# Spectral filter and gated convolution: all eight batches relaid on chip by in-place transposes instead of through DRAM

## The chip, the cores and the metric

The kernel runs on one core of one Trainium2 chip. The metric is device time in microseconds (us) of one execution; the time of a kernel is the median of its runs. A time with a profile comes from one execution that the hardware profiler recorded, and its span runs from the first to the last instruction.

TensorE (PE) multiplies matrices from SBUF into PSUM, which has eight banks of 512 f32 per partition here. VectorE (DVE) and ScalarE (ACT) read PSUM, and copy results out of it. GpSimd (POOL) works on SBUF only and also issues DMAs, as does SyncE (SP). Each engine works through its own instructions in the order in which they were written.

## The reference

```python
def _attn_ref(x, filt_r, filt_i):               # x: (8, 3200, 256) float32
    X = np.fft.rfft(x, axis=1)                  # filters: (1601, 256)
    Y = X * (filt_r + 1j * filt_i)[None, :, :]
    return np.fft.irfft(Y, n=x.shape[1], axis=1)

def _moe_ref(x, w_val, conv_w, w_out):          # x is the result above
    gate_pre = ...                              # causal convolution, 5 taps per channel
    gate = 1.0 / (1.0 + np.exp(-gate_pre))
    return gate * (x @ w_val) @ w_out           # 256 x 256 weights
```

Each of eight batches is filtered along its 3200 positions in the frequency domain, and the result goes through a sigmoid gate (a five-tap convolution), a 256 x 256 product and an output product.

## The kernel before

The length 3200 is written as 100 x 32, so that each transform is two small ones with a relayout between them. One batch goes through these stages (the names are those of the functions and of the planner's tasks):

- `load_x` (L450, DMA issued on POOL): four loads of 100 x 8 x 256 into `xt`, converted to bf16.
- `s1` (L717, PE): eight pairs of matmuls with the cosine table; `so` copies each out of PSUM (ACT or DVE). `turn` (L736, DVE): four in-place transposes of 32 x 32 blocks of 32-bit words, each word two neighbouring channels in bf16. `s2` (L745, PE) in seven chunks, copied out to `xs`.
- `zed` (L765 or L768): the product with the filter, per chunk two multiplications of 128 x 1024 bf16 (the seventh chunk is half as wide). In batches 1 to 7 five chunks of seven are on POOL (L768) and two on DVE (L765); in batch 0 all are on DVE.
- `inva` (L778, PE): first inverse stage, seven chunks; `ue` copies each out of PSUM.
- The inverse relayout. In batches 1 to 7 `ue` copies to `u`, `wr` (L818) writes `u` to a DRAM scratch `escr` with seven DMAs, and `lv` (L825) reads it back in the other layout into `vt` with eight DMAs, all on SP's queue. `lv` waits for all seven writes. In batch 0 alone (`turned`) `ue` copies into the scratch tile `yt` in pieces of four channels, and `turn2` (L808, DVE) transposes to `vt` with four instructions that write each 32-bit word 512 bytes from the last.
- `ib` (L831, PE): 64 small matmuls whose weights are slices of `vt`; `ye` (L841, ACT) copies out to `yt`, the filtered signal.
- `conv` (L861), `gate` (L870, ACT), `val` (L877) and `gv` (L887, DVE), `outp` (L897) and `oe` (a copy to `o`), `store` (L916, L919, DMAs on SP).

All copies out of PSUM go through one helper, so they have the lines L443 (ACT) and L445 (DVE) and are told apart by their tiles. The helper `copy` is an ACTIVATE on ACT and a tensor copy on DVE.

The order on all engines is laid out ahead: `tasks` lists every piece of work with a cost, a rank (`period`, `off`, `step`, `set`, `move` in `CFG`), buffers that it takes and gives, and PSUM banks; `Plan.run` goes through time, always starts the ready task with the lowest rank on a free engine, and the code is emitted in that order. It also decides which copies go to ACT and which to DVE. Nothing is reordered at run time.

The table `ci_t` of the last inverse stage is computed near the start by some forty small POOL instructions (`ci_dve`, L642 to L691), in two variants, one for each layout of `vt`.

Of the kernel before, what the change touches and what calls it, by code (L numbers as in the profile page):

```python
# [39 lines left out]
    off=dict(lx=-8.88, s1=1.96, t1=3.63, s2=6.86, xs=21.17, z=1.67, ia=13.06, ue=3.93,  # L40
         t2=-19.97, wr=-19.93, lv=18.75, ib=22.57, ye=6.81, cv=37.79, ga=-0.5, vl=26.91,
         gv=22.89, op=11.0, oe=-2.84, st=22.73),
    step=dict(lx=1.84, s1=0.42, t1=3.74, t2=1.66, s2=0.13, xs=1.06, z=0.38, ia=0.73,
         ue=2.68, wr=0.9, lv=1.54, ib=0.85, ye=2.8, cv=3.99, ga=2.94, vl=1.98, gv=0.32,
         op=0.98, oe=3.24, st=4.45),
    dup=('SP', 'SP'),
    set=dict(ey=-16.46, tab=16.6, tabs=3.8, ci=7.23, dg=29.54, fd=-37.59, w=27.01),
    move={('cv', 0): 2.79, ('cv', 1): -11.55, ('cv', 2): -0.2, ('cv', 3): -1.85, ('cv', 4):
# [34 lines left out]
    stay=0,  # L83
    hold=4.78,
# [11 lines left out]
class Plan:  # L96
# [14 lines left out]
    def run(self):  # L111
# [28 lines left out]
        while left or any(lines.values()):  # L140
# [29 lines left out]
            if best is None:  # L170
                later = [ready_at[n] for n in ready if ready_at[n] > now + 1e-9]
                later += [v for v in free.values() if v > now + 1e-9]
                later += [g[0] for g in events if g[0] > now + 1e-9]
                live = [q for q in lines.values() if q]
                if live:
                    rate = 1.0 / len(live)
                    later.append(now + min(q[0][0] for q in live) / rate)
                assert later, ("stuck", sorted(ready)[:20], self.room, banks)
                then = min(later)
                for q in live:  # L180
                    q[0][0] -= (then - now) * rate
                    if q[0][0] <= 1e-9:
                        n, give = q.pop(0)[1:]
# [28 lines left out]
            if t["dma"]:  # L212
                lines[t["dma"][0]].append([t["dma"][1], n, t["give"]])
# [10 lines left out]
def tasks(cfg, B):  # L224
    plan = Plan(cfg["room"], cfg["stay"], cfg["hold"])
    turned, move = set(cfg["turned"]), cfg["move"]
# [14 lines left out]
    fixed("s1", {"POOL": 2.0}, -95, [], ("iota_b",))  # L241
# [12 lines left out]
    fixed("cid", {"POOL": 4.5}, sr["ci"], ["s1"], ("ci_dve",))  # L254
    fixed("cia", {"ACT": 0.6}, sr["ci"], ["cid"], ("ci_act",))
    fixed("cim", {"POOL": 0.5}, sr["ci"], ["cia"], ("ci_mul",))
    fixed("id", {"DVE": 0.6}, sr["ey"], ["s1"], ("eye32",))
    fixed("dg", {"ACT": 2.0}, sr["dg"], ["id"], ("diag",))
    for c, (m0, m1) in enumerate(FCUT):
        nm = m1 - m0  # L260
        for w in range(2):
            for t in range(2):
                for k in range(3):
                    fixed(f"f{c},{w},{t},{k}", {"POOL": 0.55}, -90 + c, [], ("fload", c, w, t, k),
                          dma=("SW", 0.53 if k == 0 else 0.065 * nm))
        for t in range(2):
            for w in range(2):
# [3 lines left out]
                      ("fdup", c, t, w), dma=("HW", 0.09 * nm) if by == "SP" else None)  # L271
    fixed("wl", {"POOL": 3.0}, sr["w"], [], ("wload",), dma=("SW", 1.2))
# [3 lines left out]
    for b in range(B):  # L276
        for c in range(NXC):
            add(f"lx{b},{c}", {"POOL": 0.7}, "lx", b, c if b else c - 100, [], ("load_x", b, c),
                take=("xt",), dma=("SW", 2.4))
# [7 lines left out]
        for q in range(4):  # L287
            add(f"t1{b},{q}", {"DVE": 1.16}, "t1", b, q, sos + ([f"t1{b},{q - 1}"] if q else []),
                ("turn", b, q))
        for u, (m0, nm) in enumerate(UCH):  # L290
# [8 lines left out]
            if u in cfg["pool_u"][min(b, 1)]:  # L299
                for w in range(2):  # L300
                    add(f"z{b},{u},{w}", {"POOL": 0.13 + 0.975 * nm}, "z", b, u,
# [14 lines left out]
            if b not in turned:
                add(f"wr{b},{u}", {"SP": 0.4}, "wr", b, u,
                    [f"ue{b},{u}"] + ([f"wr{b},{u - 1}"] if u else []), ("wr", b, u),
                    take=("e",) if u == 0 else (), give=("u",), dma=("HW", 0.45 * nm))
        if b in turned:  # L320
            for q in range(4):
                add(f"t2{b},{q}", {"DVE": 1.77}, "t2", b, q, [f"ue{b},{u}" for u in range(NU)]
                    + ([f"t2{b},{q - 1}"] if q else []), ("turn2", b, q),
# [639 lines left out]
```

## Time and profile before

| | us |
|---|---|
| median of three runs | 344.0 |
| the runs | 341.51, 344.0, 346.14 |
| the profiled execution | 341.4 |
| its span | 339.7 |
| PE, DVE, ACT, POOL busy in it | 270.1, 268.0, 243.4, 192.4 |

The span leaves 1.7 us of the execution outside it. The granted TensorE clock was 0.938 of full speed on the mean. In rows of the profile, a group shows line, engine, operation, output<-inputs, shapes and count, then busy us and mean ns of one, then the idle time of its engine just before them and what ended it.

### The profile page before, as it was taken

How to read it: one execution, taken by the hardware profiler on the slowest of the kernel's cores; microseconds unless marked ns; L12 is line 12 of the kernel's file. 1: busy time of each engine (PE TensorE's matmuls, PEld its weight loads, DVE VectorE, ACT ScalarE, POOL GpSimd, SP SyncE). 2: the span in 40 equal slices, each digit the busy share in tenths (PEclk: the TensorE clock that was granted, in tenths of full speed). 3: DMA queues.
4: the chain of work that ended last, by engine and by line, in shares of the span. 5: the costliest groups of instructions: out<-in, count | busy, mean ns of one | idle time of the engine just before them, and what ended most of it. 6: DMA issues, size and time to landing. Idle time of an engine off the chain costs nothing.

```text
span 339.7 us, 11239 instructions
## 1 busy us (share of the span) xinstructions
PE 270.1 (80%) x4804; PEld 165.0 (49%) x4804; DVE 268.0 (79%) x340; ACT 243.4 (72%) x318; POOL 192.4 (57%) x214
## 2 busy tenths in 40 slices
PE   2645387769778788977897979987889989989894
PEld 0133124445345443544445646645545666657663
DVE  4887477999999898995699669789997464877482
ACT  2984287968786775834996967896984979546864
POOL 8487885498995879858356540598499610000000
PEclk9999995899995897985998999999997999999999
DMA  6999869704579645999589716786684694687436
GB/s 110 167 209 218 181 87 192 128 20 159 182 224 234 157 152 183 273 221 248 200 178 301 213 67 217 273 285 213 186 261 173 220 309 145 226 298 282 179 138 249
DMA packets 47690, 67.57 MB, mean 199 GB/s; under 512 B 5209, under 2 KB 31705, under 8 KB 47641
## 3 DMA queue, kind: packets, MB, share of 16 engines
q1 hardware_dynamic: 40648, 51.79, 45.1%
q0 software_dynamic: 6992, 15.08, 25.3%
q8 instruction: 37, 0.61, 0.7%
q14 instruction: 13, 0.10, 0.1%
HBM read 42.08 MB, written 38.14 MB: 236 GB/s over the span
## 4 chain that ended last, share of the span: by engine, by line
PE 37%; DMA 25%; DVE 17%; ACT 9%; issue 7%; POOL 2%; SPq 1%; DVEq 0%; ACTq 0%; POOLq 0%
DMA vt<-escr 9%; PE ps L877 8%; PE ps L897 8%; DMA out_dram<-o 7%; DVE z L765 6%; PE ps L861 6%; ACT yt L841 6%; PE ps L717 5%; PE ps L778 4%; PE ps L831 4%; DMA f_t<-in_filt_i_dram 3%; DMA f_t<-in_filt_r_dram 3%; DVE vt L808 2%; DMA f_t<-f_t 2%; PE ps L745 2%
## 5 line engine op out<-in xcount | busy, mean ns | idle before, releaser
L768 POOL TENSOR_TENSOR z<-xs,f_t 128x1024 bf16<-128x1024 bf16 (+1 forms) x70 | 140.0, 2029 | 52.5 <-DVE xs L445 27.9
L887 DVE TENSOR_TENSOR gv<-ps,gt 128x512 bf16<-128x512 f32 (+1 forms) x112 | 65.4, 625 | 21.2 <-ACT gt L870 13.1
L870 ACT ACTIVATE gt<-ps 128x1024 bf16<-128x1024 f32 (+1 forms) x56 | 49.6, 934 | 22.7 <-PE ps L861 20.0
L877 PE MATMUL ps<-yt,wv_t 128*128 128x512 bf16 (+1 forms) x224 | 58.0, 368 | 6.0 <-DVE o L445 2.9
L841 ACT ACTIVATE yt<-ps 128x800 bf16<-128x800 f32 (+1 forms) x72 | 54.3, 783 | 8.0 <-PE ps L831 7.0
L897 PE MATMUL ps<-wo_t,gv 128*128 128x256 bf16 x384 | 57.6, 279 | 0.6 <-DVE o L445 0.3
L717 PE MATMUL ps<-xt,cf_t 100*128 100x512 bf16 x128 | 48.2, 483 | 12.0 <-DMA xt<-in_x_dram 10.6
L765 DVE TENSOR_TENSOR z<-xs,f_t 128x1024 bf16<-128x1024 bf16 (+1 forms) x42 | 51.0, 1257 | 5.4 <-DMA xt<-in_x_dram 3.9
L443 ACT ACTIVATE so<-ps 128x1024 bf16<-128x1024 f32 x43 | 42.7, 1029 | 8.6 <-PE ps L717 8.6
L897 PEld LDWEIGHTS <-gv 128*128 128x128 bf16 x384 | 40.0, 116 | 15.7 <-issue 5.9
L831 PE MATMUL ps<-ci_t,vt 104*128 104x100 f16 (+1 forms) x512 | 37.7, 227 | 8.9 <-DMA vt<-escr 4.9
L861 PE MATMUL ps<-yt,dg_t 32*32 32x512 bf16 (+1 forms) x2240 | 39.6, 363 | 5.7 <-issue 3.3
L443 ACT ACTIVATE u<-ps 128x1024 bf16<-128x1024 f32 (+1 forms) x33 | 31.7, 975 | 16.6 <-DMA escr<-u 8.4
L831 PEld LDWEIGHTS <-vt 104*128 104x128 bf16 (+1 forms) x512 | 31.8, 109 | 23.5 <-issue 8.2
L443 ACT ACTIVATE o<-ps 128x512 f32<-128x512 f32 (+1 forms) x58 | 33.2, 586 | 13.4 <-PE ps L897 10.2
L778 PE MATMUL ps<-z,a_t 64*64 64x256 bf16 x416 | 31.2, 302 | 13.6 <-ACT so L443 3.6
L445 DVE COPY o<-ps 128x512 f32<-128x512 f32 (+1 forms) x46 | 29.8, 661 | 12.9 <-PE ps L897 7.1
L736 DVE STREAM_TRANSPOSE so<-so 128x1024 f32<-128x1024 f32 x32 | 38.7, 1235 | 0.2
L778 PE MATMUL ps<-z,b_t 64*64 64x256 bf16 x416 | 30.0, 294 | 7.5 <-DVE z L765 7.5
L443 ACT ACTIVATE xs<-ps 128x1024 bf16<-128x1024 f32 (+1 forms) x31 | 30.0, 978 | 8.2 <-PE ps L745 5.1
L861 PEld LDWEIGHTS <-dg_t 32*32 32x32 bf16 x2240 | 26.6, 88 | 17.8 <-issue 13.1
L445 DVE CAST xs<-ps 128x1024 bf16<-128x1024 f32 (+1 forms) x25 | 28.1, 1132 | 7.2 <-PE ps L745 6.6
(101 smaller groups left out, 242.2 us busy)
## 6 DMA issues: line engine op xcount, KB each, us to landing
out_dram<-o SPq DMA_DIRECT2D x48, 512.0 KB
xt<-in_x_dram POOLq DMA_DIRECT2D x32, 400.0 KB, 8.5
vt<-escr SPq DMA_DIRECT2D x56, 208.0 KB
escr<-u SPq DMA_DIRECT2D x42, 256.0 KB
out_dram<-o SPq DMA_DIRECT2D x8, 128.0 KB
f_t<-f_t SPq DMA_DIRECT2D x4, 224.0 KB
escr<-u SPq DMA_DIRECT2D x7, 128.0 KB
f_t<-f_t SPq DMA_DIRECT2D x4, 192.0 KB
```

The source lines that it names most:

```text
L443: nc.scalar.activation(dst, src, AF.Copy, **kw)
L445: nc.vector.tensor_copy(dst, src)
L717: nc.tensor.matmul(PS[:, bk[h], :], lhsT=cf_t[0:L].rearrange("p h c i -> p (h c i)"), rhs=xv[:, DQ // 2 * h:DQ // 2 * h + DQ // 2], start= ...
L765: nc.vector.tensor_tensor(z[:, k, :, 0:nm * D], xs_[:, :, 0:nm * D], f[:, k], op=ALU.mult)
L768: (nc.vector if e == "DVE" else nc.gpsimd).tensor_tensor(z[:, w, :, 0:nm * D], xs_[:, :, 0:nm * D], f[:, w], op=ALU.mult)
L778: nc.tensor.matmul(PS[64 * h:64 * h + 64, bk[t], D * a:D * a + D], lhsT=tab[rows, h, m0 + a, :], rhs=z[rows, w, h, D * a:D * a + D], start ...
L831: nc.tensor.matmul(PS[:, bk[n], L * a:L * a + L], lhsT=VT[0:k, RC * i + a, 128 * dh:128 * dh + 128], rhs=ci_t[0:k, int(b in turned), :], s ...
L841: nc.scalar.activation(y.rearrange("p h (a r) -> p h a r", r=R)[:, :, :, RC * i:RC * i + RC], st.pop(("ib", b, i, hs))[:, :, 0:RC * L].rea ...
L861: nc.tensor.matmul(PS[32 * j:32 * j + 32, bk[2 * x + half], 0:n], lhsT=dg_t[rows, dh, k, :], rhs=y[rows, dh, n0 + k:n0 + k + n], start=(k ...
L877: nc.tensor.matmul(PS[:, bk[0], 0:n], lhsT=wv_t[:, j & 1, dh, h, :], rhs=y[:, dh, H + n0:H + n0 + n], start=(dh == 0), stop=(dh == 1))
L887: nc.vector.tensor_tensor(st["GV", b, j][:, h, 0:n], PS[:, st.pop(("vl", b, j, h)), 0:n], st["G", b, j][:, h, 0:n], op=ALU.mult)
L897: nc.tensor.matmul(PS[:, bk[0], D * a:D * a + D], lhsT=gv_[:, r, 2 * h + a:n:4], rhs=wo_t[:, j & 1, r, :], start=(r == 0), stop=(r == 1))
```

## The change

Every batch gets the same inverse relayout, on chip. `ue` writes from PSUM straight into a tile `v` of 128 partitions x 128 channel pairs x 32 x 2 in bf16: channels c and c + 128 lie in one 32-bit word, and the words of one pair are 32 in a row, 26 of them filled. Consecutive elements of one copy go to consecutive pairs, so they land 128 bytes apart. `pads` (POOL) zeroes the other six words of each pair, 768 words per partition, before. `turn2` is then four transposes of 128 x 1024 words in place, contiguous in both directions. `ib` takes as weights, for one half of the channels, 128 elements 128 bytes apart, and uses all 128 partitions instead of 104. `wr`, `lv`, the DRAM scratch, `u`, `vt` and their buffers are gone; `v` has two buffers.

Six chunks of seven are multiplied on POOL in batches 1 to 7 (both halves, `pool_z`); the half-wide seventh stays on DVE. Batch 0 stays on DVE. The table for `ci_t` has one variant and is computed on DVE by 27 small instructions instead of on POOL. `xt` has five buffers (six before), `z` three (four before). The planner's costs, its model of DMA queues and all its ranks are other numbers, so the order on every engine differs.

```diff
-    turned=(0,),
-    pool_u=((), (0, 2, 3, 5, 6)),
-    room=dict(xt=6, so=2, xs=3, z=4, u=4, e=2, v=8, y=2, g=4, gv=4, o=3),
-    period=7.05,
+    pool_z=((), ((0, 0), (0, 1), (1, 0), (1, 1), (2, 0), (2, 1), (3, 0), (3, 1), (4, 0), (4,
+         1), (5, 0), (5, 1))),
+    room=dict(xt=5, so=2, xs=3, z=3, v=2, y=2, g=4, gv=4, o=3),
+    period=6.93,
...
+            add(f"ue{b},{u}", ev(512 * nm), "ue", b, u, [f"ia{b},{u}", f"pd{b}"], ("ue", b, u),
+                free=[(f"ia{b},{u}", (0, 1))])
+        add(f"pd{b}", {"POOL": 0.9}, "pd", b, 0, [], ("pads", b), take=("v",))
+        for q in range(4):
+            add(f"t2{b},{q}", {"DVE": 1.16}, "t2", b, q, [f"ue{b},{u}" for u in range(NU)]
+                + ([f"t2{b},{q - 1}"] if q else []), ("turn2", b, q))
...
+    def pads(e, b):
+        v = st["V", b] = vpool.tile([128, 128, 32, 2], BF16, name="v")
+        nc.gpsimd.memset(v[:, :, NS:32, :].rearrange("p c m h -> p c (m h)").bitcast(FP32), 0.0)
+
     def ue(e, b, u):
         m0, nm = UCH[u]
         src = st.pop(("ia", b, u))[:, :, 0:nm * D]
-        u_ = upool.tile([128, 2, 2 * D], BF16, name="u")
-        copy(e, u_[:, :, 0:nm * D], src)
-        st["U", b, u] = u_
+        dst = st["V", b][:, :, 2 * m0:2 * m0 + 2 * nm, :].rearrange(
+            "p c (t a) h -> p t a h c", t=2)
+        copy(e, dst.rearrange("p t a h c -> p (t a) h c"),
+             src.rearrange("p t (a h c) -> p t a h c", h=2, c=128)
+             .rearrange("p t a h c -> p (t a) h c"))
...
     def turn2(e, b, q):
-        w = D // 8
-        ut = st["UT", b][...].bitcast(FP32)
-        src = bass.AP(tensor=ut.tensor, offset=ut.offset + NS * w * q,
-                      ap=[list(ut.ap[0]), [2 * NS, DQ // 4], [1, 2], [2, 32]])
-        dst = (VT[...].rearrange("p r d -> p (r d)").bitcast(FP32)
-               .rearrange("p (r n) -> p n r", r=R)[:, w * q:w * q + w]
-               .rearrange("p (q w) r -> p q w r", w=2))
-        nc.vector.transpose(dst, src)
+        v = (st["V", b][:, 32 * q:32 * q + 32].rearrange("p c m h -> p (c m h)").bitcast(FP32))
+        nc.vector.transpose(v, v)
...
-    def ib(e, b, i, hs, bk):
-        k = 128 if b in turned else NV
-        for n, dh in enumerate(hs):
+    def ib(e, b, i, bk):
+        for dh in range(2):
             for a in range(RC):
-                nc.tensor.matmul(PS[:, bk[n], L * a:L * a + L],
-                                 lhsT=VT[0:k, RC * i + a, 128 * dh:128 * dh + 128],
-                                 rhs=ci_t[0:k, int(b in turned), :], start=True, stop=True)
+                nc.tensor.matmul(PS[:, bk[dh], L * a:L * a + L],
+                                 lhsT=st["V", b][:, :, RC * i + a, dh], rhs=ci_t[...],
+                                 start=True, stop=True)
```

How the order moved shows on three engines. On SP, a piece from the later half of the kernel before (`escr<-u` are the writes to the scratch, `vt<-escr` the reads, `out_dram<-o` the stores):

```order
L825 DMA vt<-escr 104x1024
L916 DMA out_dram<-o 128x1024
L825 DMA vt<-escr 104x1024 x6
L818 DMA escr<-u 128x4x256
L825 DMA vt<-escr 104x1024
L818 DMA escr<-u 128x4x256
L916 DMA out_dram<-o 128x1024
L919 DMA out_dram<-o 128x256
```

The writes and reads are gone, and after the filter copies SP has nothing but stores. On DVE, about two thirds into the kernel before, the products of one chunk (`z`) stand between copies and gate products (`gv`):

```order
L887 TENSOR_TENSOR gv<-ps,gt 128x512 x2
L765 TENSOR_TENSOR z<-xs,f_t 128x1024 x2
L445 COPY o<-ps 128x512 x2
L445 CAST u<-ps 128x2x256
L887 TENSOR_TENSOR gv<-ps,gt 128x512 x2
L445 CAST so<-ps 128x64x16
L445 COPY o<-ps 128x512
```

The changed kernel's DVE at about the same place, with the half-wide product of the seventh chunk, the forward transposes (`so`) and the four new ones (`v`):

```order
L720 TENSOR_TENSOR z<-xs,f_t 128x2x256 x2
L691 STREAM_TRANSPOSE so<-so 128x16x2x32
L815 TENSOR_TENSOR gv<-ps,gt 128x512 x2
L815 TENSOR_TENSOR gv<-ps,gt 128x128
L691 STREAM_TRANSPOSE so<-so 128x16x2x32
L815 TENSOR_TENSOR gv<-ps,gt 128x512 x2
L419 COPY o<-ps 128x256
L419 CAST xs<-ps 128x1024 x2
L755 STREAM_TRANSPOSE v<-v 128x1024 x3
L815 TENSOR_TENSOR gv<-ps,gt 128x512 x4
```

The wide products have left this engine, and three transposes in a row now stand ahead of gate products. On POOL, where the products of batch 3 stand in the changed kernel, with a load of x and the zeroing of `v` for a later batch among them (the tile numbers are the builder's own, one to a buffer in use):

```order
L723 TENSOR_TENSOR z_2199<-xs_1998,f_t_63 128x1024
L723 TENSOR_TENSOR z_2298<-xs_2182,f_t_63 128x1024 [waits DVE_49]
L742 MEMSET v_2343 128x128x6 [waits PE_49]
L723 TENSOR_TENSOR z_2298<-xs_2182,f_t_63 128x1024
L723 TENSOR_TENSOR z_2447<-xs_2241,f_t_63 128x1024 [waits DVE_49,PE_49,Pool_49]
L424 DMA xt_2480<-in_x_dram 100x2048 [waits DMASW7_49]
L723 TENSOR_TENSOR z_2447<-xs_2241,f_t_63 128x1024
```

Before, POOL had ten products per batch and no zeroing among them but that of eight columns of `yt`; now the zeroing of `v` waits for the `ib` matmuls (PE) of two batches earlier, with products queued behind it.

More of the change, by code (lines that the diff above doesn't have):

```diff
@@ L175, in run @@
                 if live:
-                    rate = 1.0 / len(live)
-                    later.append(now + min(q[0][0] for q in live) / rate)
+                    pk = sum(q[0][3] for q in live)
+                    later.append(now + min(q[0][0] * pk / q[0][3] for q in live))
                 assert later, ("stuck", sorted(ready)[:20], self.room, banks)
@@ L180, in run @@
                 for q in live:
-                    q[0][0] -= (then - now) * rate
+                    q[0][0] -= (then - now) * q[0][3] / pk
+                for q in live:
                     if q[0][0] <= 1e-9:
-                        n, give = q.pop(0)[1:]
+                        _, n, give, _ = q.pop(0)
                         done(n, then + self.LAT)
@@ L212, in run @@
             if t["dma"]:
-                lines[t["dma"][0]].append([t["dma"][1], n, t["give"]])
+                lines[t["dma"][0]].append([t["dma"][1], n, t["give"], t["dma"][2]])
             else:
@@ L277, in tasks @@
         for c in range(NXC):
-            add(f"lx{b},{c}", {"POOL": 0.7}, "lx", b, c if b else c - 100, [], ("load_x", b, c),
-                take=("xt",), dma=("SW", 2.4))
+            ring = ("ring",) * 29
+            add(f"lx{b},{c}", {"POOL": 0.58}, "lx", b, c if b else c - 100, [], ("load_x", b, c),
+                take=("xt",) + ring, give=ring, dma=("SW", 2.15, 325))
         for j in range(NCH):
@@ L298, in tasks @@
                 free=[(f"s2{b},{u}", (0, 1))])
-            if u in cfg["pool_u"][min(b, 1)]:
+            by = ["POOL" if (u, w) in on_pool else "DVE" for w in range(2)]
+            if by == ["DVE", "DVE"]:
+                add(f"z{b},{u}", {"DVE": 0.06 + 0.545 * nm}, "z", b, u, [f"xs{b},{u}"] + fl,
+                    ("zed", b, u, 2), give=("xs",))
+                zs = [f"z{b},{u}"]
+            else:
                 for w in range(2):
-                    add(f"z{b},{u},{w}", {"POOL": 0.13 + 0.975 * nm}, "z", b, u,
+                    add(f"z{b},{u},{w}", {"POOL": 0.13 + 0.975 * nm} if by[w] == "POOL" else
+                        {"DVE": 0.03 + 0.29 * nm}, "z", b, u,
                         [f"xs{b},{u}"] + fl + ([f"z{b},{u},0"] if w else []),
@@ L316, in tasks @@
[L316 to L323, printed above, removed]
-                    take=("v",) * NCH if q == 0 else (), give=("y",) if q == 3 else ())
@@ new lines, in tasks @@
+            add(f"ue{b},{u}", ev(512 * nm), "ue", b, u, [f"ia{b},{u}", f"pd{b}"], ("ue", b, u),
[4 more added lines that the diff above has]
+                + ([f"t2{b},{q - 1}"] if q else []), ("turn2", b, q))
+        for i in range(NCH):
+            add(f"ib{b},{i}", {"PE": 0.353}, "ib", b, i,
+                ["cim"] + ([f"ib{b},{i - 1}"] if i else [f"t2{b},{q}" for q in range(4)]),
+                ("ib", b, i), banks=2, take=("y",) if i == 0 else (),
+                give=("v",) if i == NCH - 1 else (), mode=0)
+            add(f"ye{b},{i}", {"ACT": act(800)}, "ye", b, i, [f"ib{b},{i}"],
+                ("ye", b, i), free=[(f"ib{b},{i}", (0, 1))])
@@ L696, in ci_mul @@
     def ci_mul(e):
-        for n in range(2):
-            tsg(ci_t[:, n, :], g["sx"][:, n, :], g["wt"][:, n:n + 1], ALU.mult)
+        ts(ci_t[...], g["sx"][...], g["wt"], ALU.mult)
     def eye32(e):
```

200 lines of the change are left out of this document (66 added, 134 removed), and 58 rows, old and new, of the table move.

## The prediction

> **What bounds the kernel now.** I read the page first: busy shares, then the chain of work that ended last.
>
> ```profile
> span 339.7 us, 11239 instructions
> PE 270.1 (80%) x4804; PEld 165.0 (49%) x4804; DVE 268.0 (79%) x340; ACT 243.4 (72%) x318; POOL 192.4 (57%) x214
> ...
> PE 37%; DMA 25%; DVE 17%; ACT 9%; issue 7%; POOL 2%; SPq 1%; DVEq 0%; ACTq 0%; POOLq 0%
> DMA vt<-escr 9%; PE ps L877 8%; PE ps L897 8%; DMA out_dram<-o 7%; DVE z L765 6%; PE ps L861 6%; ACT yt L841 6%; PE ps L717 5%; PE ps L778 4%; PE ps L831 4%; DMA f_t<-in_filt_i_dram 3%; DMA f_t<-in_filt_r_dram 3%; DVE vt L808 2%; DMA f_t<-f_t 2%; PE ps L745 2%
> ```
>
> No engine is full. A quarter of the chain is DMA: reading the scratch back is its largest single line. Second, the busy time by stretches, cut where POOL begins its first product (65.3) and ends its last (273):
>
> ```profile
> core 0: us, PE busy (x) PEld busy (x) DVE busy (x) ACT busy (x) POOL busy (x), PEclk, DMA share, GB/s
> 0.00:65.30 65.30, 37.82 (x340) 18.67 (x340) 46.34 (x76) 41.95 (x63) 44.70 (x123) 0.92 0.90 164
> 65.30:273.00 207.70, 173.47 (x3218) 104.85 (x3210) 180.63 (x197) 157.21 (x195) 147.53 (x89) 0.93 0.68 201
> 273.00:339.70 66.70, 58.76 (x1260) 41.50 (x1254) 41.02 (x70) 44.27 (x61) 0.21 (x2) 0.99 0.63 228
> ```
>
> PE looks fullest, but its matmuls are pipelined and a waiting one counts as busy. DVE and ACT share all copies out of PSUM, so I sum on their mean: (268.0 + 243.4)/2 = 255.7 us busy, 84.0 idle. In the middle stretch they are busy for (180.6 + 157.2)/2 = 168.9 of 207.7 (81%), in the tail 42.6 of 66.7 (64%). Third, the waits, to see whose idle time a DMA ends:
>
> ```profile
> PE ps L717 <- DMA xt<-in_x_dram: 10.6, 5, 6.7
> ACT u L443 <- DMA escr<-u: 8.4, 2, 6.5
> ACT so L443 <- PE ps L717: 8.6, 11, 2.4
> ACT yt L841 <- PE ps L831: 7.0, 9, 2.6
> PEld L831 <- DMA vt<-escr: 6.2, 4, 2.4
> PE ps L831 <- DMA vt<-escr: 4.9, 4, 2.1
> DVE o L445 <- DMA out_dram<-o: 4.1, 3, 2.4
> DVE so L445 <- PE ps L717: 3.7, 6, 1.2
> ACT o L443 <- DMA out_dram<-o: 2.6, 2, 1.6
> POOL z L768 <- DVE xs L445: 27.9, 6, 13.3
> POOL z L768 <- ACT xs L443: 24.5, 9, 7.6
> ```
>
> Last, the groups with shapes kept apart (the first of them over the time after 65.3 alone):
>
> ```profile
> L765 DVE TENSOR_TENSOR z<-xs,f_t 128x1024 bf16<-128x1024 bf16 x28 | 42.4, 1551 | 0.0
> ...
> L768 POOL TENSOR_TENSOR z<-xs,f_t 128x1024 bf16<-128x1024 bf16 x56 | 124.1, 2238 | 47.8 <-ACT xs L443 24.5 <-DVE xs L445 23.2
> L841 ACT ACTIVATE yt<-ps 128x800 bf16<-128x800 f32 x56 | 47.2, 843 | 8.0 <-PE ps L831 7.0
> L736 DVE STREAM_TRANSPOSE so<-so 128x1024 f32<-128x1024 f32 x32 | 38.7, 1235 | 0.2
> L443 ACT ACTIVATE u<-ps 128x1024 bf16<-128x1024 f32 x28 | 28.7, 1039 | 14.6 <-DMA escr<-u 8.4 <-PE ps L778 5.6 <-ACT o L443 0.3
> L445 DVE CAST u<-ps 128x1024 bf16<-128x1024 f32 x14 | 17.0, 1219 | 3.5 <-PE ps L778 1.6 <-ACT yt L841 1.2 <-ACT gt L870 0.3
> L450 POOL DMA_DIRECT2D xt<-in_x_dram x32 | 17.9, 561 | 19.4 <-PE ps L717 13.1 <-PE ps L877 4.4 <-POOLq L947 0.8
> L808 DVE STREAM_TRANSPOSE vt<-yt 128x1024 f32<-128x1024 f32 x4 | 7.6, 1939 | 2.1 <-PE ps L831 2.0
> L443 ACT ACTIVATE yt<-ps 128x1024 bf16<-128x1024 f32 x4 | 4.1, 1024 | 0.4 <-PE ps L778 0.4
> L445 DVE CAST yt<-ps 128x1024 bf16<-128x1024 f32 x2 | 2.5, 1226 | 3.3 <-PE ps L778 3.3
> L765 DVE TENSOR_TENSOR z<-xs,f_t 128x512 bf16<-128x512 bf16 x2 | 0.8, 418 | 0.0
> L496 POOL MEMSET ident<- 128x128 f32 x1 | 0.2, 210 | 0.0
> ```
>
> A wide product takes DVE 1551 ns on the mean while POOL multiplies too. The timeline shows why: DVE's pair began just behind a POOL product and took 4.34 us, and in batch 0, with no POOL product beside it, five took 3.10 us.
>
> ```profile
> 154.31 2.13 POOL L768 TENSOR_TENSOR z<-xs,f_t 128x1024 bf16<-128x1024 bf16 x1
> ...
> 178.38 4.66 POOL L768 TENSOR_TENSOR z<-xs,f_t 128x1024 bf16<-128x1024 bf16 x2 [3.30 <-ACT xs L443]
> ...
> 25.57 3.10 DVE L765 TENSOR_TENSOR z<-xs,f_t 128x1024 bf16<-128x1024 bf16 x5 [0.45 <-DMA f_t<-f_t]
> ...
> 179.25 4.34 DVE L765 TENSOR_TENSOR z<-xs,f_t 128x1024 bf16<-128x1024 bf16 x2
> ```
>
> **The change, part by part** (DVE and ACT time together, halved at the end).
>
> Transposes: 28 more at 1.235 = +34.6; batch 0's four go from 1.939 to 1.235, -2.8. Together +31.8. In-place and contiguous is nearest to L736, which is in place with words 8 bytes apart; none is seen to slow beside POOL.
>
> Products: 28 wide ones leave DVE, -42.4. Fourteen half-wide ones stay: free, 14 x 0.418 = 5.9; each of the 7 pairs behind a POOL product as at 179 us, 4.34 - 2 x 0.62 = 3.1 more, 27.6. The 28 removed cost 42.4 instead of 28 x 0.62 = 17.4, so 25.0/3.1 = 8 of 14 pairs were held; at that share I take 18.3. Together -24.1 (ends -36.5 and -14.8).
>
> Copies: the order gives ACT four `so` and two `xs` more and DVE six fewer, 6 x (1.04 - 1.22) = -1.
>
> The copies `ue` into `v`: every element lands 128 bytes from the last, which no row shows for a copy. Low end: batch 0's `yt` copies, which jump after every four elements, took 1.024 on ACT and 1.226 on DVE, as much as the plain `u` copies. High end: the transposes L808, which write each word 512 bytes on, took 0.704 more than L736. On DVE (15 wide, 4 half: 17) that is 0 to 12.0, on ACT (33 and 4: 35) 0 to 24.6. A gain is excluded, since the same elements pass. I take 0 on both: the `yt` rows are the same operation from PSUM on the same two engines, L808 is another operation. The high end is the first rival. The Trainium skill ("Advanced Engine Details and Errata", section Memory Cachelines) says that SBUF has 16-byte lines and that accesses which each touch another line pay a penalty. By that rule both engines pay, as L808 may show, and the sum below would be 18.3 us higher.
>
> Sum of work: 31.8 - 24.1 - 1 = +6.7, or +3.4 per engine. The 27 small instructions of the table on DVE fall into the first stretch, where DVE idles 19 of 65 us; at 0.15 each they are 4 us, which I put at nothing: the filter's arrival covers them, and without it the first `ib` would be up to 4 late.
>
> PE: the weights of `ib` are elements 128 bytes apart, 512 loads. I price that at nothing, because ACT takes 0.843 to copy out what eight such matmuls give, so PE may slow to 0.105 each; beyond that it adds to the wait of `ye` on PE (7.0 now). Ends 0 and +7.
>
> DMA: 49 writes and 56 reads leave SP, whose queue then holds only stores. Idle time that a DMA ends on ACT and DVE is 8.4 + 2.6 + 4.1 = 15.1, or 7.6 per engine. PE's waits for `vt` (11.1) and for x starve ACT and DVE in turn: their waits for `s1` and `ib` are 8.6 + 3.7 + 7.0 = 19.3; I take half, 4.8 per engine. So -12.4. The ends: 0, if other waits close the gaps, and about -24, if nearly half of the 16% of the chain (54 us) in `vt<-escr` and `out_dram<-o` goes.
>
> Tail: behind the last `inva` of batch 7 the order leaves 27 `gv`, 7 copies `o` and four transposes on DVE where 38 and 19 stood, and 12 gates on ACT where 18 stood: some 16 us of work, 8 per engine, moves from a stretch that is 64% busy into one that is 81% busy. 8/0.64 - 8/0.81 = 2.6 less.
>
> POOL: between its first and last product it has 84 x 2.13 (the timeline's lone product; 2.24 is the mean with DVE's wide products beside it) = 179, some 15 loads at 0.561 = 8.4, and six zeroings of 768 words, 0.21 (the row for 128 words) to 1.26 (six times that) each, 5: about 193 us where 147.5 were. The zeroing of `v` for the next batch waits for `ib` of the batch before, with up to half a batch of products behind it, and `inva` on PE waits for those. I take +5 idle per engine (0 to +27, below).
>
> Sum: 255.7 + 3.4 + 84.0 - 12.4 - 2.6 + 5 = 333.1; with 1.7 outside the span 334.8. The profiled execution took 341.4, 0.8% below the median of 344.0, so I say 335 against 344 for the runs.
>
> **Rivals.** *The strided copies cost what L808 costs*, on ACT too: +36.6 together, 18.3 per engine, 353; with ACT's queue now fuller than DVE's, 355. Slower by 2% (351) from 0.43 us more per wide copy on both. For it: the one row with such a write. Against it: the `yt` rows. If only DVE pays, 6 more: 341.
>
> *POOL becomes the bound.* Its 193 us must fit between first and last product. With a first stretch of 64, a tail of 54 and 1.7 outside, 335 leaves 215, so POOL must be busy 90%, where it now is 71%. At 80% the stretch takes 241 and the kernel 361; it is slower by 2% below 84%. For it: the 52 us that POOL waits for `xs` now, in an order with more slack. Against it: the copies to `xs` come up to three chunks ahead.
>
> *More of the chain goes than I count*: the -24 end, and no new wait on POOL: 334.8 - 11.6 - 5 = 318.
>
> *The DRAM trip was hidden anyway*: other waits close every gap, 334.8 + 12.4 = 347.
>
> **How the numbers follow.** Two per cent (337 to 351) is about what a measurement can tell from no change. Forecast 335: chance 0.36 (own range 323 to 345; faster 0.6, same 0.38). Only DVE pays, 341: 0.08 (faster 0.25, same 0.7). More goes, 318: 0.10 (faster). Both pay, 355: 0.23 (slower 0.7). POOL bound, 361: 0.17 (slower 0.85). Hidden, 347: 0.06 (slower 0.3). Faster: 0.22 + 0.02 + 0.10 + 0.02 of the rest = 0.36. Slower: 0.16 + 0.145 + 0.02 + 0.015 = 0.34. Same: 0.30. The range 318 to 364 leaves out about half of the third case and the worst of the fourth and fifth, some 0.18.
>
> **What would show it.** The copies to `v` at 1.03 on ACT and 1.22 on DVE, or 0.7 more; transposes of `v` at 1.2; DVE's half products between 0.42 and 2; POOL's busy share between its products, and its waits for `xs` and for `ib` at the zeroing; no `escr` in the chain; waits of `o` for stores gone; `ib` loads near 0.105. Wrong would be: copies at 1.9, POOL at 80% or less with `inva` waiting for it, or a `ye` that waits for `ib` much longer than 7 us in all.

## The result, and the profile after

The changed kernel takes 502.25 us (median of four runs, 500.28 to 502.92) where the kernel before takes 342.78 (341.51 to 346.14): a ratio of 1.462, 95% interval 1.450 to 1.475. The forecast was 335 with a range up to 364. The profiled execution has a span of 499.9 us. First its page: the span, the busy shares and the chain of work that ended last.

```profile
span 499.9 us, 10965 instructions
PE 333.8 (67%) x4772; PEld 199.1 (40%) x4804; DVE 323.9 (65%) x372; ACT 377.4 (75%) x319; POOL 224.6 (45%) x193
...
PE 35%; ACT 33%; DVE 16%; issue 9%; DMA 5%; POOL 2%; ACTq 0%; another core or an unknown queue 0%; DVEq 0%; POOLq 0%
ACT v L417 24%; DVE v L419 12%; PE ps L760 7%; PE ps L825 6%; PE ps L789 6%; PE ps L805 6%; PE ps L733 5%; PE ps L672 4%; ACT gt L798 3%; DMA xt<-in_x_dram 2%; ACT o L417 2%; ACT xs L417 2%; PE ps L700 1%; ACT so L417 1%; DMA f_t<-in_filt_r_dram 1%
```

DMA has fallen from 25% of the chain to 5%, as the change says, and no `escr` is left. But 36% of the chain, 180 us, is now the copies `ue` into `v`, on ACT and DVE. The groups with shapes kept apart name their price (columns: group, count, busy us, mean ns of one, idle before):

```profile
L417 ACT ACTIVATE v<-ps 128x1024 bf16<-128x1024 f32 x33 | 157.5, 4789 | 14.6 <-PE ps L733 14.6
L417 ACT ACTIVATE v<-ps 128x512 bf16<-128x512 f32 x4 | 9.9, 2472 | 5.5 <-PE ps L733 5.5
L419 DVE CAST v<-ps 128x1024 bf16<-128x1024 f32 x15 | 71.0, 4734 | 16.4 <-PE ps L733 12.2 <-ACT gt L798 4.2
L419 DVE CAST v<-ps 128x512 bf16<-128x512 f32 x4 | 9.8, 2447 | 1.3 <-PE ps L733 1.3
...
L755 DVE STREAM_TRANSPOSE v<-v 128x1024 f32<-128x1024 f32 x32 | 38.3, 1222 | 17.6 <-ACT v L417 17.6
...
L720 DVE TENSOR_TENSOR z<-xs,f_t 128x512 bf16<-128x512 bf16 x16 | 11.1, 735 | 2.0 <-ACT xs L417 2.0
L723 POOL TENSOR_TENSOR z<-xs,f_t 128x1024 bf16<-128x1024 bf16 x84 | 177.4, 2135 | 114.5 <-ACT xs L417 79.0 <-DVE xs L419 35.4
```

A wide copy takes 4.79 us on ACT and 4.73 on DVE, where a plain one took 1.04 and 1.22. The four groups sum to 157.5 + 9.9 + 71.0 + 9.8 = 248.2 us. The transposes that follow, at 1.222, cost what was forecast. Next the view of the tile `v` that lists who waited for it (us, times):

```profile
who waited for it (us, times):
  POOL v L742: 45.6, 6
  PE ps L672: 33.1, 12
  ACT yt L768: 30.0, 37
  PE ps L700: 29.6, 9
  PE ps L760: 21.5, 8
  DVE v L755: 17.6, 6
  PE ps L733: 16.0, 6
  PE ps L789: 15.4, 7
  PE ps L805: 14.8, 6
```

PE stands still 33.1 + 29.6 + 21.5 + 16.0 + 15.4 + 14.8 = 130.4 us for work on `v`, and mostly before matmuls that do not read it: `s1` (L672), `s2` (L700) and `val` (L805) wait for PSUM banks, which the copy gives free at its end, and a copy of 4.8 us holds its two that much longer. Last the busy time in three stretches, the first and the last of them as long as those shown of before, to within 4 us:

```profile
core 0: us, PE busy (x) PEld busy (x) DVE busy (x) ACT busy (x) POOL busy (x), PEclk, DMA share, GB/s
0.00:65.00 65.00, 29.28 (x244) 11.77 (x245) 39.79 (x93) 49.57 (x43) 32.63 (x77) 1.00 0.84 141
65.00:430.00 365.00, 252.04 (x3554) 149.27 (x3581) 237.77 (x228) 282.18 (x224) 183.43 (x111) 0.77 0.26 72
430.00:500.00 70.00, 52.48 (x982) 38.02 (x982) 46.31 (x53) 45.69 (x54) 8.53 (x5) 0.91 0.30 119
```

The loss lies in the middle, 365 us where 208 stood, and there POOL is busy only half of the time (183.4 us): it was not the bound.

### The profile page after: what moved, and what is told of

Same layout as the page of the kernel before. It is cut to its first block, busy times and chain, and to the rows that moved or that the text cites. A ratio compares the mean times of both kernels' runs of the same rounds, so it can differ in the third digit from the quotient of the medians.

```text
span 499.9 us, 10965 instructions
## 1 busy us (share of the span) xinstructions
PE 333.8 (67%) x4772; PEld 199.1 (40%) x4804; DVE 323.9 (65%) x372; ACT 377.4 (75%) x319; POOL 224.6 (45%) x193
## 2 busy tenths in 40 slices
DMA packets 17056, 43.70 MB, mean 87 GB/s; under 512 B 3696, under 2 KB 6896, under 8 KB 17008
## 3 DMA queue, kind: packets, MB, share of 16 engines
q1 hardware_dynamic: 10016, 27.93, 14.3%
## 4 chain that ended last, share of the span: by engine, by line
PE 35%; ACT 33%; DVE 16%; issue 9%; DMA 5%; POOL 2%; ACTq 0%; another core or an unknown queue 0%; DVEq 0%; POOLq 0%
ACT v L417 24%; DVE v L419 12%; PE ps L760 7%; PE ps L825 6%; PE ps L789 6%; PE ps L805 6%; PE ps L733 5%; PE ps L672 4%; ACT gt L798 3%; DMA xt<-in_x_dram 2%; ACT o L417 2%; ACT xs L417 2%; PE ps L700 1%; ACT so L417 1%; DMA f_t<-in_filt_r_dram 1%
## 5 line engine op out<-in xcount | busy, mean ns | idle before, releaser
L723 POOL TENSOR_TENSOR z<-xs,f_t 128x1024 bf16<-128x1024 bf16 x84 | 177.4, 2135 | 114.5 <-ACT xs L417 79.0
L417 ACT ACTIVATE v<-ps 128x1024 bf16<-128x1024 f32 (+1 forms) x37 | 167.4, 4539 | 20.2 <-PE ps L733 20.2
L419 DVE CAST v<-ps 128x1024 bf16<-128x1024 f32 (+1 forms) x19 | 80.8, 4252 | 17.7 <-PE ps L733 13.4
L672 PE MATMUL ps<-xt,cf_t 100*128 100x512 bf16 x128 | 54.6, 537 | 41.0 <-ACT v L417 26.6
L768 ACT ACTIVATE yt<-ps 128x800 bf16<-128x800 f32 x64 | 54.8, 876 | 30.3 <-PE ps L760 30.0
L805 PE MATMUL ps<-yt,wv_t 128*128 128x512 bf16 (+1 forms) x192 | 61.7, 418 | 17.6 <-DVE v L419 8.1
L825 PE MATMUL ps<-wo_t,gv 128*128 128x256 bf16 x384 | 70.7, 321 | 2.2 <-ACT v L417 1.1
L760 PE MATMUL ps<-ci_t,v 128*128 128x100 f16 x512 | 55.0, 270 | 22.7 <-ACT v L417 12.9
L760 PEld LDWEIGHTS <-v 128*128 128x128 bf16 x512 | 53.0, 203 | 33.7 <-issue 28.5
L789 PE MATMUL ps<-yt,dg_t 32*32 32x512 bf16 (+1 forms) x2240 | 50.9, 460 | 18.5 <-ACT v L417 10.3
L700 PE MATMUL ps<-so,w_t 64*64 64x256 bf16 x416 | 27.5, 349 | 39.6 <-ACT v L417 26.1
L755 DVE STREAM_TRANSPOSE v<-v 128x1024 f32<-128x1024 f32 x32 | 38.3, 1222 | 17.6 <-ACT v L417 17.6
L733 PE MATMUL ps<-z,a_t 64*64 64x256 bf16 x416 | 36.5, 352 | 18.3 <-ACT v L417 12.8
```

What stands on the lines that cost most here:

```text
L417: nc.scalar.activation(dst, src, AF.Copy, **kw)
L419: nc.vector.tensor_copy(dst, src)
L672: nc.tensor.matmul(PS[:, bk[h], :], lhsT=cf_t[0:L].rearrange("p h c i -> p (h c i)"), rhs=xv[:, DQ // 2 * h:DQ // 2 * h + DQ // 2], start= ...
L723: (nc.vector if e == "DVE" else nc.gpsimd).tensor_tensor(z[:, w, :, 0:nm * D], xs_[:, :, 0:nm * D], f[:, w], op=ALU.mult)
L733: nc.tensor.matmul(PS[64 * h:64 * h + 64, bk[t], D * a:D * a + D], lhsT=tab[rows, h, m0 + a, :], rhs=z[rows, w, h, D * a:D * a + D], start ...
L760: nc.tensor.matmul(PS[:, bk[dh], L * a:L * a + L], lhsT=st["V", b][:, :, RC * i + a, dh], rhs=ci_t[...], start=True, stop=True)
```

## The experiments

Four theories stood at the start for the 3.7 us that a copy takes more. *Line theory*: a price for each change to another 16-byte line of SBUF. *Stride theory*: the step of 128 bytes itself is unlucky. *Half-word theory*: the price is for writing 2 bytes of a 4-byte word alone. *Crowding theory*: ACT and DVE, both writing far apart, hold each other up. Each kernel's interval is against runs of the kernel before on the same chip.

### price: the operations by themselves

This kernel leaves the whole computation out and runs only copies of 1024 elements from PSUM, transposes and groups of 48 matmuls, each with other steps between elements. Three lines of it: lone bf16 elements 128 bytes apart, pairs of them 128 bytes apart, and f32 elements 128 bytes apart.

```diff
+        for _ in range(4): nc.scalar.activation(far(d, 64), s8, AF.Copy)
+        for _ in range(4): nc.scalar.activation(run(d, 2), srun(2), AF.Copy)
+        for _ in range(4): nc.scalar.activation(far(df, 32), s8, AF.Copy)
...
```

> The kernel does only copies, transposes and weight loads, in groups of four to sixteen, and leaves out the whole computation. Line theory (a price per new 16-byte line, whatever is written): copies of 1024 elements stay near 1.0 us on ACT and 1.2 us on DVE up to 8 bytes apart, and take about 4.7 us from 16 bytes on, whether the elements have 2 or 4 bytes and whatever the stride. Stride theory (multiples of 128 bytes fall on one bank): about 4.7 us at 128, 256 and 512 bytes, and clearly less at 132 and 144. Half-word theory (a 2-byte write alone in its line is a read and a write): 4.7 us for 2-byte elements, about 1.9 us for 4-byte ones as in the transposes before, and half or less for pairs. Crowding theory (the copies are slow because the other engines use SBUF): under 2.5 us everywhere here, where each engine works alone. Weight loads 128 bytes apart: about 90 ns from matmul to matmul where adjacent weights take 44.

The groups, one line of the kernel to each; first ACT with bf16 8, 16, 128 and 132 bytes apart, then in pairs 128 bytes apart, then f32 128 bytes apart; DVE beside a strided ACT; transposes contiguous and with words 512 bytes apart:

```profile
L65 ACT ACTIVATE d<-ps 128x1024 bf16<-128x1024 f32 x4 | 9.7, 2432 | 0.1
L66 ACT ACTIVATE d<-ps 128x1024 bf16<-128x1024 f32 x4 | 18.8, 4692 | 0.1
L69 ACT ACTIVATE d<-ps 128x1024 bf16<-128x1024 f32 x4 | 18.9, 4721 | 0.1
L70 ACT ACTIVATE d<-ps 128x1024 bf16<-128x1024 f32 x4 | 18.7, 4685 | 0.1
L74 ACT ACTIVATE d<-ps 128x1024 bf16<-128x1024 f32 x4 | 4.1, 1025 | 0.1
L81 ACT ACTIVATE d<-ps 128x1024 f32<-128x1024 f32 x4 | 7.5, 1877 | 0.1
L115 DVE CAST dtwo<-ps 128x1024 bf16<-128x1024 f32 x16 | 19.6, 1224 | 0.5
L107 DVE STREAM_TRANSPOSE d<-d 128x1024 f32<-128x1024 f32 x4 | 5.0, 1246 | 0.1
L109 DVE STREAM_TRANSPOSE d<-d 128x1024 f32<-128x1024 f32 x4 | 8.7, 2182 | 0.1
```

The same view gives the rest of the steps (mean us of one copy):

| step between elements, bytes | 2 | 4 | 8 | 16 | 32 | 64 | 128 | 132 | 512 |
|---|---|---|---|---|---|---|---|---|---|
| ACT, bf16 | 1.02 | 1.30 | 2.43 | 4.69 | 4.44 | 4.61 | 4.72 | 4.69 | 4.72 |
| DVE, bf16 | 1.22 | 1.29 | 2.42 | 4.68 | 4.43 | 4.60 | 4.71 | 4.67 | 4.71 |
| ACT, f32 | | 1.02 | 1.07 | 1.96 | | | 1.88 | 1.98 | 1.88 |
| DVE, f32 | | 1.22 | 1.23 | 1.95 | | | 1.87 | 1.97 | 1.87 |

For lone bf16 elements the price nearly doubles from 4 to 8 and from 8 to 16 bytes and then stays within 4.43 to 4.72 us: it goes by 16-byte lines touched. With lone halves of words a line costs 4692/1024 = 4.6 ns (2432/512 = 4.8 with two halves in it), with whole words 1962/1024 = 1.9. Pairs of halves, written one right after the other, take 1.025 us, no more than contiguous ones, as if the two halves were joined before the line is paid for. Why a lone half costs more than a whole word isn't shown. So neither of the two holds alone: half-word theory is right on what is dear, and line theory on what is counted. "Line theory" in the expectations of the later runs means this: so much for each line, by what is written to it. Stride theory falls: 128 is no worse than 132 or 16. Crowding falls as well: DVE's contiguous copies took 1.224 beside a strided ACT, and with both strided a copy took 4.94 and 4.91, 4 to 5% more than alone.

### runs8: the same places, visited in another order

```diff
+        dst = st["V", b][:, :, 2 * m0:2 * m0 + 2 * nm, :].rearrange("p c m h -> p c (m h)")
+        copy(e, dst.rearrange("p (t c) n -> p t c n", t=2),
+             src.rearrange("p t (c n) -> p t c n", c=64))
```

> The copies to v write the same addresses as the changed kernel, but in runs of eight neighbouring elements instead of one element every 128 bytes, which permutes the data. If the order of the writes is the whole cause, the copies take 1.0 us on ACT and 1.2 us on DVE, and the kernel falls from 502 us to what was forecast without it, 335 us (318 to 361). If the transposes, the weight loads 128 bytes apart or POOL's products carry a part, it stays over 370 us with the copies at 1.0 to 1.3 us.

It took 331.52 us (two runs, 331.12 to 331.92), ratio 0.964 (0.948 to 0.979). The copies to `v`, which write the same addresses in runs of eight elements, fell to 1.03 on ACT and 1.22 on DVE. The channels end up permuted within `v`, so this kernel leaves the right result out; every engine has the same instructions. Only the order in which a copy writes was changed, so the 171 us come from it.

### pair and pair_again: both halves of a word one after the other

```diff
-        dst = st["V", b][:, :, 2 * m0:2 * m0 + 2 * nm, :].rearrange(
-            "p c (t a) h -> p t a h c", t=2)
-        copy(e, dst.rearrange("p t a h c -> p (t a) h c"),
-             src.rearrange("p t (a h c) -> p t a h c", h=2, c=128)
-             .rearrange("p t a h c -> p (t a) h c"))
+        dst = st["V", b][:, :, 2 * m0:2 * m0 + 2 * nm, :].rearrange("p c m h -> p m c h")
+        copy(e, dst, src.rearrange("p t (a h c) -> p t a h c", h=2, c=128)
+             .rearrange("p t a h c -> p (t a) c h"))
```

The elements go where the changed kernel puts them; only the innermost loop is the half `h` now, and PSUM is read 512 bytes to and fro for it.

> The copies write channel c and c + 128 one after the other, so each 128-byte step writes one whole word in two halves; PSUM is read 512 bytes apart instead. Line theory: half the lines, copies of about 2.5 us, and the kernel near 400 us. Stride theory: the same. Half-word theory: if the two halves are joined, 1.2 us or less per copy and the kernel near 340 us; if they are not joined, 4.7 us as before and 500 us. If reading PSUM so costs as much, no change either.

It took 331.68 us (two runs), ratio 0.964 (0.947 to 0.981). A second time, with four runs:

> The kernel with the two halves of each word written one after the other, once more, for an interval beside its variants. Line theory: 331.7 as before, ratio 0.964. Nothing else is tested.

330.96 us (329.59 to 333.87), ratio 0.973 (0.955 to 0.990). The page and the groups of the first:

```profile
span 328.8 us, 10965 instructions
PE 273.5 (83%) x4772; PEld 180.5 (55%) x4804; DVE 272.8 (83%) x372; ACT 250.4 (76%) x319; POOL 225.3 (69%) x193
```

```profile
L766 ACT ACTIVATE yt<-ps 128x800 bf16<-128x800 f32 x64 | 53.7, 859 | 13.1 <-PE ps L758 12.3 <-DVE o L419 0.2
L758 PEld LDWEIGHTS <-v 128*128 128x128 bf16 x512 | 52.5, 206 | 8.9 <-DVE v L753 3.1 <-issue 2.5 <-DVE gv L813 0.2
L417 ACT ACTIVATE v<-ps 128x1024 bf16<-128x1024 f32 x33 | 35.7, 1083 | 10.7 <-PE ps L733 10.3
L720 DVE TENSOR_TENSOR z<-xs,f_t 128x512 bf16<-128x512 bf16 x16 | 22.0, 1412 | 0.0
L419 DVE CAST v<-ps 128x1024 bf16<-128x1024 f32 x15 | 18.4, 1224 | 9.8 <-PE ps L733 8.8 <-ACT gt L796 0.9
L742 POOL MEMSET v<- 128x768 f32 x8 | 6.1, 757 | 12.2 <-PE ps L758 12.2
```

The copies cost 1.08 and 1.22 us: the case of joined halves, and not the 2.5 us of line theory as it was first stated, for which each line costs the same whatever is written. The kernel is faster than before: everything else of the change, taken together, is a gain of 3 to 4% (1 to 5% by the two intervals), and comes out 3 to 4 us under the forecast.

### pitch33: another step, still alone

```diff
-        v = st["V", b] = vpool.tile([128, 128, 32, 2], BF16, name="v")
+        v = st["V", b] = vpool.tile([128, 128, 33, 2], BF16, name="v")
```

The transposes go on taking 32 words of each row, now of 33.

> Each pair of channels gets 33 words instead of 32, so the elements of a copy lie 132 bytes apart instead of 128, and the weights too; nothing else differs. Stride theory: copies of 1.0 to 1.9 us and a kernel of 335 to 370 us. Line theory and half-word theory: copies of 4.7 us, 500 us.

With elements 132 bytes apart it took 493.91 us (two runs, 491.99 to 495.83), ratio 1.436 (1.410 to 1.462). Its row of tile `v` shows min, median and max of all copies on ACT:

```profile
L417 ACT ACTIVATE v<-ps x37: 2440/4734/5051, 31.4 to 451.9; 128x1024 bf16<-128x1024 f32 x33, 128x512 bf16<-128x512 f32 x4
```

Stride theory is out in the kernel too. The 8 us by which it beats the changed kernel are about what the weights give below, under pair33.

### mix: half the dose

```diff
+        if b % 2:
+            dst = st["V", b][:, :, 2 * m0:2 * m0 + 2 * nm, :].rearrange("p c m h -> p m c h")
...
+        else:
+            dst = st["V", b][:, :, 2 * m0:2 * m0 + 2 * nm, :].rearrange(
+                "p c (t a) h -> p t a h c", t=2)
...
```

> Half dose: batches 1, 3, 5, 7 write as pair does, batches 0, 2, 4, 6 as the changed kernel does. If each costly copy adds its own time, half of the 170.6 us between pair and the changed kernel: 417. If a batch's copies are covered up to some point (slack of the neighbouring batch), less: 380 to 400. If one slow batch holds up its neighbours as well, more: 440. Copies: 4.7 to 4.8 us in the even batches, 1.05 to 1.22 in the odd ones.

It took 411.63 us (two runs), ratio 1.207 (1.186 to 1.228). Halfway between pair_again and the changed kernel is (331.0 + 502.3)/2 = 416.6, so each costly batch adds about the same, (411.6 - 331.0)/4 = 20 us for the first four and (502.3 - 411.6)/4 = 23 for the others: the neighbouring batches cover little of it. The time lies 5 us below the 417 of the first case expected. The copies to `v`, summed over their four groups, took 153.8 us, halfway between pair's 59.3 and the changed kernel's 248.2 too.

### pair33: pair with weights 132 bytes apart

The edits of pair and pitch33 together.

> Pair with 33 words per channel pair in place of 32, so that the 512 ib weight loads read elements 132 bytes apart. Line theory for the copies, and the measured load price (91 ns per matmul at 128 bytes, 60 at 132): PEld at about 160 ns in place of 206, PE some 512 x 0.03 = 15 us less, and of ACT's 12.3 us of waiting for ib up to all of it gone; if the kernel is bound there, 326 to 330. Rival, the weights are hidden behind the copies out of PSUM: 331.7 within 0.5%. Copies to v stay at 1.08 on ACT and 1.22 on DVE in both.

It took 323.77 us (322.24 to 325.14), ratio 0.949 (0.935 to 0.963). Four runs of pair_again on the same chip lay between 329.59 and 333.87: the two do not overlap, and the difference is 7.2 us. That is 2 us below the 326 expected at best, although ACT's copies to `v` took 1.14 us and not 1.08. It is the fastest version here. Its groups, to be held against the first two of pair's:

```profile
L767 ACT ACTIVATE yt<-ps 128x800 bf16<-128x800 f32 x64 | 52.7, 849 | 5.9 <-PE ps L759 3.9
L759 PEld LDWEIGHTS <-v 128*128 128x128 bf16 x512 | 41.3, 163 | 9.4 <-issue 3.0 <-DVE v L754 2.9 <-DVE gv L814 0.2
```

A weight load fell from 206 ns to 163, and ACT's wait for `ib` from 12.3 us to 3.9. The rival, weights hidden behind the copies out of PSUM, is refuted. The groups of 48 matmuls in price agree (weights 4, 16, 128, 132 and 256 bytes apart):

```profile
L117 PE MATMUL ps<-r,d 128*128 128x100 bf16 x48 | 2.3, 208 | 0.0
L119 PE MATMUL ps<-r,d 128*128 128x100 bf16 x48 | 3.1, 224 | 0.0
L122 PE MATMUL ps<-r,d 128*128 128x100 bf16 x48 | 4.6, 255 | 0.0
L123 PE MATMUL ps<-r,d 128*128 128x100 bf16 x48 | 3.0, 223 | 0.0
L125 PE MATMUL ps<-r,d 128*128 128x100 bf16 x48 | 6.2, 307 | 0.0
```

With weights 4 bytes apart 48 matmuls take 2.3 us. By the timeline the next group starts 2.12 us after this one, so it is 2.12/48 = 44 ns from one matmul to the next, at 8 bytes as well. At 16 bytes it is 61, at 132 bytes 60, at 128 bytes 91 and at 256 bytes 125 (there the granted clock fell to 0.5 halfway; it was 1.00 in the others). For weights, unlike for writes, the step of 128 bytes is worse than 132.

### word: the price moved to the transposes

```diff
-        v = st["V", b] = vpool.tile([128, 128, 32, 2], BF16, name="v")
+        v = st["V", b] = vpool.tile([128, 32, 128, 2], BF16, name="v")
```

The copies write half words 4 bytes apart, and the transposes read and write words 512 bytes apart.

> The other way to avoid the price on the copies: v as [32 m][128 channel pairs][2], so a copy writes half words 4 bytes apart (eight of a 16-byte line's elements come as four in a row, then the other four) and the transposes take words 512 bytes apart, in place; ib's weights lie 4 bytes apart. Line theory, from the prices measured alone: copies 1.30 (ACT 35 x 0.27 more than plain, DVE 17 x 0.07: +11), transposes 2.18 in place of 1.22 (32 x 0.96: +31), together 21 per engine more than pair, less some 6 of ib's waits: 331.0 + 21 - 6 = 346, between 340 and 352. Half-word theory without lines (each lone half word costs 3.6 ns more wherever it lands): copies stay at 4.7, above 480. A theory that the costly copies were dear because of the 32-word rows of v and not of the step between elements: 331.

It took 359.21 us (355.54 to 360.62), ratio 1.046 (1.036 to 1.056).

```profile
L754 DVE STREAM_TRANSPOSE v<-v 128x1024 f32<-128x1024 f32 x32 | 71.1, 2263 | 0.9 <-ACT v L417 0.9
L417 ACT ACTIVATE v<-ps 128x1024 bf16<-128x1024 f32 x33 | 44.3, 1342 | 14.3 <-PE ps L733 13.9
L419 DVE CAST v<-ps 128x1024 bf16<-128x1024 f32 x15 | 19.8, 1318 | 7.0 <-PE ps L733 6.5 <-ACT gt L797 0.3
```

The single prices are those of price (1.34 and 1.32 for 1.30, 2.26 for 2.18), so the line price holds here, and the two rivals that gave 331 and over 480 are out. The time is 13 us above what I made of the prices, and outside the bounds. The 6 us that I took off for cheaper weights did not come: a weight load fell to 108 ns from 206, but ACT still waited 14.3 us for `ib`, in 12 waits where pair had 33. The rest fits the rule of the mean. DVE's busy time rose by 33.7 us to 306.4 of 356.3, ACT's by 6.3. Half of their sum is 20.0; the span rose by 27.9. Taking the mean of the two engines was too mild here, where the extra work falls on the fuller one.

### pair_five and six: the products alone

pair_five is pair with the share of before: chunks 1 and 4 whole on DVE, chunk 6 on POOL. The planner lays the order out anew with the same ranks.

```diff
-    pool_z=((), ((0, 0), (0, 1), (1, 0), (1, 1), (2, 0), (2, 1), (3, 0), (3, 1), (4, 0), (4,
-         1), (5, 0), (5, 1))),
+    pool_z=((), ((0, 0), (0, 1), (2, 0), (2, 1), (3, 0), (3, 1), (5, 0), (5, 1), (6, 0), (6, 1))),
```

> Pair with the products shared as in the kernel before: chunks 0, 2, 3, 5, 6 on POOL, 1 and 4 whole on DVE, the order by the same numbers. The products term of the forecast (24.1 us of DVE time, 12 per engine): 331.7 + 12 = 344. POOL theory (POOL, busy about 90% between its products, holds the kernel): no slower, 325 to 332. In between, some 337, if DVE's extra work falls in part into its idle time.

It took 352.89 us (352.45 to 354.47), ratio 1.036 (1.027 to 1.045): 21.9 us more than pair_again, where 12 were forecast. POOL theory is not borne out: with POOL's busy time down from 225.9 us to 188.2 the kernel is slower, though in an order that changed as well.

```profile
L719 DVE TENSOR_TENSOR z<-xs,f_t 128x1024 bf16<-128x1024 bf16 x40 | 64.4, 1649 | 1.0 <-DMA f_t<-f_t 1.0
```

Forty wide products for 64.4 us stand where pair has 12 for 7.9 and 16 halves for 22.0; DVE's busy time is 300.4 us, 27.7 more than in pair_again, ACT's 5.1 more. Again half the sum (16.4) is less than what the span gained (22.9).

six is the kernel before, DRAM detour and all, with six chunks on POOL.

```diff
-    pool_u=((), (0, 2, 3, 5, 6)),
+    pool_u=((), (0, 1, 2, 3, 4, 5)),
```

> The kernel before, with the detour through DRAM kept, but six product chunks of seven on POOL. If DVE's product time was what counted there (24.1 us less on DVE, 12 per engine): 332. If the DRAM detour's waits set the pace: 341 to 344. If POOL becomes the bound in an order not made for it: above 346.

It took 368.1 us (366.54 to 369.35), ratio 1.070 (1.061 to 1.079). DVE's work fell as expected, from 268.0 to 251.0 us, and yet the kernel lost 24: the third of the cases expected. POOL's row for all its products, and two waits of others:

```profile
L768 POOL TENSOR_TENSOR z<-xs,f_t x84: 2107/2130/2308, 64.4 to 311.8; 128x1024 bf16<-128x1024 bf16 x84
```

```profile
DVE gv L887 <- PE ps L877: 27.4, 16, 7.7
...
PE ps L778 <- DVE z L765: 21.0, 12, 4.9
```

The products took POOL 177.3 us for 140.7 before, 36.6 more, and the stretch from the first to the end of the last grew from 207.7 us to 249.5, 41.8 more; the stretch behind it shrank from 66.7 us to 52.2, so the kernel lost less than that. `inva` waits 21.0 us for products (8.7 before), and what follows it comes late (`gv` for `val`, 27.4 for 7.8). Pair has the same 84 products in 225 us, in an order laid out for them. So this run doesn't price the products; it shows that a sixth chunk on POOL was no gain without its order. In pair_five, too, the order is one made for the other share, and its 21.9 is an upper value for the term.

## Why the prediction was wrong, point by point

**The step that failed is the term of the `ue` copies into `v`**, "I take 0 on both", with 0.704 us a copy as its high end. They took 3.75 us more on ACT (4.789 for 1.039) and 3.51 more on DVE. Both rows that I bounded it by were of another kind. The `yt` copies jump after every four elements, so their halves come joined (in price, runs of four take 1.023). The transposes L808 write whole words: 1939/1024 = 1.9 ns each, the price of a line with a whole word. A lone half pays 4.6. Beyond the copies' own size, the sum was too mild as well: 248.2 - 59.3 = 188.9 us more of copying on the two engines cost 171 us of span, 0.9 us for each us, where the sum over their mean counts a half. The row that was nearest by its step (words 512 bytes apart) differed in the size of what was written, and I noted that neither row was the operation itself and still let them close the range.

**How 3.7 us a copy became 171 us.** Between pair's profile and the changed kernel's the span differs by 499.9 - 328.8 = 171.1. The mean busy time of ACT and DVE rose from (272.8 + 250.4)/2 = 261.6 to (323.9 + 377.4)/2 = 350.7, by 89.1; the copies alone, 248.2 for 35.7 + 2.5 + 18.4 + 2.7 = 59.3, explain 94.5, and DVE's half products became cheaper by 10.9/2, perhaps since they met fewer products of POOL. The other 82 are idle time of the two engines: PE waited 130.4 us for work on `v` (6.8 in pair), and what both copy next comes from PE. PE's matmuls also took longer, those of `inva` 344 to 352 ns for 287 to 297, at a granted clock of 0.82 for 0.97; how much of the 82 us that is was not separated. Mix shows that the loss is nearly proportional to the number of costly batches.

**What of the rest came right** is read from pair, where the failed term is gone: 331.0 to 331.7 against 335. Mean busy 261.6 for 259.1 forecast, idle 67.2 for 74.0.

- Transposes: 1.219 to 1.222 us each for 1.235.
- Products: 14 half-wide ones were forecast at 18.3 us in all, and 16 took 22.0, two of them in batch 0 for 0.7: 21.3 for 18.3, 3 us too little and inside the bounds of 5.9 and 27.6. What the share of products is worth in time may have been set too low: 12 us were counted, and pair_five loses up to 21.9.
- Weights of `ib`: I took 0 of 0 to +7. Pair33 gives 7.2 back, and its weights are not contiguous either, so the high end was the nearer one, or still too low. The argument that PE may slow to 0.105 us a matmul before ACT notices failed: with such weights a matmul took 0.091 in price, and in pair ACT waited 12.3 us for `ib` all the same (7.0 before). Why it waits at that pace isn't shown.
- DRAM trip: no `escr` is left in the chain, and the DMA queues move 43.70 MB for 67.57. How much of the idle time this alone took off was not separated.
- POOL: its wait at the zeroing was there (12.2 us in pair), and did not decide. From the row of its products in pair_again,

```profile
L723 POOL TENSOR_TENSOR z<-xs,f_t x84: 2115/2140/2331, 57.4 to 280.1; 128x1024 bf16<-128x1024 bf16 x84
```

the stretch lasts from 57.4 to 282.2, 224.8 us; the 193 us of work that I counted fill 86% of it, not 90%. It is 10 us longer than the 215 forecast. The stretch ahead of it (57.4 us for 64) and the tail behind it (328.4 - 282.2 = 46.2 for 54) are shorter by 14 together and made up for it. So it is luck in part that pair came so near to 335.

The rival that the copies cost what L808 costs had the right place and the wrong size: 18.3 us forecast, about 171 measured. The 0.43 us a copy beside it, from which the kernel would be slower by 2%, does not follow from the sum, which gives (350.9 - 334.8)/26 = 0.62. The rule that I set beside it, the Trainium skill's "Advanced Engine Details and Errata", section Memory Cachelines, says that SBUF has 16-byte lines and that an access which goes to another line each time pays. Price agrees with it (the price stops growing at 16 bytes), and it was the better guide than the nearest rows. The same section asks for at least two hits on a line to absorb the latency; here the measurement differs and decides: two lone halves in each line still took 2.42 us on DVE and 2.43 on ACT, where contiguous copies took 1.22 and 1.02.

## What to carry to other kernels

When a copy scatters, count the 16-byte lines that it touches, and ask whether it completes a 32-bit word each time: a lone 2-byte write cost 4.6 ns a line here, a whole word 1.9, and the cure was to exchange two loops of the access pattern. When no row of the profile has the operation in question, its bound must come from a row with the same element size and step, or stay open upwards. And once that is mended, look at what reads the tile: weights 132 instead of 128 bytes apart gave another 2%.

## What the runs showed of the hardware that I had not expected

- A copy's time depends on the order in which it visits the same addresses: 4.79 us with the two halves of a word 128 elements apart in time, 1.08 with one right behind the other.
- ACT and DVE pay the same for lone halves (4.72 and 4.71 us), though contiguous copies differ (1.02 and 1.22).
- Transposes in place with words 512 bytes apart took 2.18 us; strided only where they wrote, or only where they read, 1.90 each; contiguous 1.25.
- Matmuls go by the step between their weights: 44 ns from one matmul to the next at 4 bytes, 61 at 16, 60 at 132, 91 at 128, 125 at 256.
- The granted clock of PE moved in ways that busy time does not explain: in the changed kernel it was 0.77 of full speed in the middle stretch, where PE was busy 252 of 365 us, and 1.00 in the first, where it was busy 29 of 65; in price it fell to 0.50 while PE never stood still. Whether that cost the changed kernel time of its own was not tried.
